# Half sums, row store, x and bz loads as items of the order lists; left rows of b by one load; head outputs of 32 columns; new lists

## The chip, the core and the metric

The kernel runs on one core of one Trainium2 chip. The metric is device time in microseconds; the median of the runs counts. TensorE (PE) multiplies, ScalarE (ACT) and VectorE (DVE) move and transform tiles, GpSimd (POOL) copies in SBUF, SyncE (SP) and, in the first part, ACT issue DMAs. PEld in the profile is the weight load of TensorE.

## What is computed

Branch A is attention with a recurrent memory: the sequence of 2048 rows (640 wide) is cut into 64 segments of 32 rows. Each segment is put behind 8 memory rows, and the first 8 rows of its output are the memory of the next one, so the 64 segments are a chain. Branch B is a gated feed-forward layer over all rows, and a gate per row mixes the two.

```python
for s in range(n_seg):
    xs = x[:, s * seg_len:(s + 1) * seg_len, :]
    h = concatenate([mem, xs], axis=1)            # 8 + 32 rows
    q, k, v = h @ Wq, h @ Wk, h @ Wv              # 32 heads of 192
    p = softmax(where(mask, q @ k.T * scale, -1e9))
    o = (p @ v) @ Wo                              # summed over heads
    mem = o[:, :M, :]
    outs.append(o[:, M:, :])
g = sigmoid((x * gate_w).sum(-1))
return g * a + (1 - g) * ((gelu(x @ w_gate) * (x @ w_up)) @ w_down)
```

All tensors are bf16.

## The kernel before

First the feed-forward part runs in four blocks of 512 rows: transposes of x, gate and up projections (L849, L852), down projection (L867, L870). Its result goes to `b_scr` in HBM, 128 rows at a time, from `brow` (store L881, on ACT's queue). The transposed x and the row gates go to HBM too. Then `segment(s)` runs 64 times.

A segment works on 32 columns, the 8 memory rows and the first 24 of its own rows. Its last 8 rows ("left" rows) can't change the memory, so they are done for four segments at once: their Q and K by "lf" items ahead of time, through HBM (`qkl`, stores L950 and L955, loads L1000 into the space of the `uT` buffers), their V (`vl`) too, and their output by `wo_left` in every fourth segment. So the score tiles have 40 columns, `R` = 32 + 8.

The 32 heads are four groups ("octets") of eight. The order of a segment's work is written out in `PROGS`, one list for each of s % 4 (called list 0 to 3 here). Each engine works its own instructions in the order in which the items add them; `_Sched` derives the waits. It also makes reads of one PSUM bank by two engines wait for each other. The items:

- ("g", n, k): projections of group n of `GROUPS`, k-th of five slices of the depth, sets of four 32-column matmuls (L1121, or L226 where the weights stay). After the last slice ACT evacuates the Q and K rows (L1141) and V (L1144).
- ("tq", i), ("tk", i): DVE transposes those rows (L1155).
- ("sc", i): mask and scores (L1163, L1171, L1176), maximum and subtraction on DVE (L1189, L1191); GpSimd then fills the left columns of Q and K for the next group (L1006, L1008).
- ("ex", i): exponent on ACT (L1201), sum, reciprocal and p on DVE (L1203 to L1208).
- ("pt", i): transposes of p (L1221, L1226) and their evacuation (L1239; for the last group L1233 on ACT and L1235 on DVE).
- ("pv", i): `pv_oct`, p times V (L1254, L1256); ACT copies the 40-column head outputs to `uT` (L1265), for the last group two thirds of them, while DVE copies the rest (L1270); GpSimd copies their 8 left columns on to `uTl` (L1273).
- ("wo", i, h): `wo_part`, output projection (L1283 into bank OB for groups 0 to 2, L1306 for the last). After ("wo", 2, 1) `half_sums` adds the two halves of the bank: ACT copies one half (L1289), DVE adds (L1292, twice). The gate column of the segment is read by ACT (L1039) after that or after "pv" of the last group, whichever item is later.
- ("lf", q, u, k), ("le", q, u, m): projections of left rows (L936, L226) and their evacuation by ACT (L941) and transpose by DVE (L943). ("vb", k): V of left rows (L1094).

At a segment's end DVE adds the last projection to the half sums (L1468) and transposes the memory rows into the next h (L1472); the next segment's first projections wait for that. `mix` (L1048, L1050) makes the output row in `bz`.

Around the lists, SP issues in this order: each weight piece that is swapped is loaded right behind the item that used its place (`swap_loads`, L645; L642 for the piece `HALF`, of which only `HX` bytes a partition are swapped); `out_store` (L1021) and `x_load` (L751) after K's last slice of group 1; `bz_load` (L1012) and, every fourth segment, `bzl_load` in four parts (L1017) after the last "g". `x_copy` (L802, GpSimd) puts the loaded x in place after the last "g".

## Time and profile before

| | |
|---|---|
| median of 3 runs | 1715.51 us (1715.17 to 1721.14) |
| the profiled execution | 1721.14 us, span 1719.3 us |
| granted TensorE clock | 0.996 |
| feed-forward part | to about 170 us |
| segments: first to last transpose of the memory rows (L1472), 62 segments | 205.9 to 1688.6 us, 23.9 us each |
| DMA | 484.99 MB, mean 282 GB/s |

In the page, busy time is the union of an engine's instructions. In the table of waits, a row names the engine and the line that waited, and the engine and line that released it. In the timeline a row has the start, the length, the engine, the line and the number of instructions merged; in brackets stands the idle time of the engine before it and its releaser. In the groups, busy time and mean length in ns come first behind the bar, then idle time of the engine before them.

### The profile page before, as it was taken

How to read it: one execution, taken by the hardware profiler on the slowest of the kernel's cores; microseconds unless marked ns; L12 is line 12 of the kernel's file. 1: busy time of each engine (PE TensorE's matmuls, PEld its weight loads, DVE VectorE, ACT ScalarE, POOL GpSimd, SP SyncE). 2: the span in 40 equal slices, each digit the busy share in tenths (PEclk: the TensorE clock that was granted, in tenths of full speed). 3: DMA queues.
4: the chain of work that ended last, by engine and by line, in shares of the span. 5: the costliest groups of instructions: out<-in, count | busy, mean ns of one | idle time of the engine just before them, and what ended most of it. 6: DMA issues, size and time to landing. Idle time of an engine off the chain costs nothing. (4 is left out here: it accounts for less than half of the span.)

```text
span 1719.3 us, 80494 instructions
## 1 busy us (share of the span) xinstructions
PE 1592.6 (93%) x39181; PEld 825.5 (48%) x31501; DVE 956.2 (56%) x2930; ACT 801.1 (47%) x1899; POOL 415.7 (24%) x1101
## 2 busy tenths in 40 slices
...
GB/s 323 319 53 137 322 299 291 320 278 285 276 303 318 278 293 282 298 304 298 280 280 290 311 299 272 290 280 320 255 288 279 314 312 269 291 265 322 274 275 240
DMA packets 273822, 484.99 MB, mean 282 GB/s; under 512 B 107686, under 2 KB 142782, under 8 KB 273470
## 3 DMA queue, kind: packets, MB, share of 16 engines
...
## 5 line engine op out<-in xcount | busy, mean ns | idle before, releaser
L1121 PE MATMUL ps<-arena 128*32 128x384 bf16 x9940 | 710.8, 329 | 20.6 <-DVE arena L1472 11.8
L226 PE MATMUL ps<-arena 128*32 128x384 bf16 x7680 | 595.3, 327 | 14.3 <-ACT arena L1039 4.4
L1121 PEld LDWEIGHTS ps<-arena 128*32 128x32 bf16 x9940 | 254.7, 96 | 392.7 <-issue 260.6
L1155 DVE STREAM_TRANSPOSE arena<-arena 128x384 bf16<-128x384 bf16 x512 | 275.3, 561 | 151.4 <-ACT arena L1141 149.8
L1141 ACT ACTIVATE arena<-ps 128x384 bf16<-128x384 f32 x512 | 237.1, 490 | 227.0 <-PE ps L1121 212.2
L1283 PE MATMUL ps<-arena 128*32 128x320 bf16 x6144 | 279.7, 301 | 15.5 <-issue 13.2
L1273 POOL COPY arena<-arena 128x96 bf16<-128x96 bf16 x256 | 163.8, 640 | 527.8 <-ACT arena L1265 480.9
L1265 ACT ACTIVATE arena<-ps 128x480 bf16<-128x480 f32 (+1 forms) x256 | 137.5, 537 | 172.3 <-PE ps L1256 160.5
L1283 PEld LDWEIGHTS ps<-arena 128*32 128x32 bf16 x6144 | 169.3, 107 | 72.9 <-issue 23.8
L1006 POOL COPY arena<-arena 128x96 bf16<-128x96 bf16 x256 | 68.9, 269 | 485.4 <-PE ps L1176 387.4
L1144 ACT ACTIVATE arena<-ps 128x384 bf16<-128x384 f32 x256 | 125.2, 489 | 104.9 <-PE ps L1121 101.6
L1189 DVE TENSOR_REDUCE arena<-ps 104x4 f32<-104x160 f32 x256 | 82.8, 323 | 141.9 <-PE ps L1176 125.1
L1203 DVE TENSOR_REDUCE arena<-ps 104x4 f32<-104x160 f32 x256 | 80.9, 316 | 103.8 <-ACT ps L1201 101.5
L1239 ACT ACTIVATE arena<-ps 128x448 bf16<-128x448 f32 x192 | 104.1, 542 | 65.9 <-PE ps L1226 64.9
L1254 PE MATMUL ps<-arena 128*64 128x160 bf16 x1536 | 118.8, 243 | 7.3 <-ACT arena L941 3.2
L1201 ACT ACTIVATE ps<-ps 104x160 f32<-104x160 f32 x256 | 74.8, 292 | 103.0 <-DVE ps L1191 103.0
L1254 PEld LDWEIGHTS ps<-arena 128*64 128x64 bf16 x1536 | 79.8, 109 | 86.4 <-issue 29.9
L936 PE MATMUL ps<-arena 128*32 128x384 bf16 x1280 | 109.4, 327 | 1.1 <-issue 1.1
L1256 PE MATMUL ps<-arena 128*64 128x64 bf16 x1536 | 102.3, 193 | 0.0
L943 DVE STREAM_TRANSPOSE arena<-arena 128x384 bf16<-128x384 bf16 x128 | 73.0, 571 | 44.2 <-ACT arena L941 43.9
L1171 PE MATMUL ps<-arena 128*40 128x40 bf16 x2048 | 68.9, 182 | 26.4 <-DVE arena L1155 24.5
L1306 PE MATMUL ps<-arena 128*32 128x160 bf16 x3072 | 71.7, 233 | 21.7 <-DVE arena L1270 16.4
...
## 6 DMA issues: line engine op xcount, KB each, us to landing
...
arena<-in_A_Wo_dram SPq DMA_DIRECT2D x205, 480.0 KB, 5.4
...
arena<-left_qk_scratch SPq DMA_DIRECT2D x126, 96.0 KB, 2.1
...
left_qk_scratch<-arena SPq DMA_DIRECT2D x30, 96.0 KB, 3.3
```

What stands on the lines that cost most here:

```text
L226: return e.add_instruction(mybir.InstMatmult(name=nm, start_tensor_calc=like["start"], stop_tensor_calc=stop, tile_size=(128, 32), tile_po ...
L936: fns.append(lambda e, outp=outp, rhs=rhs, j=j: e.matmul(outp, lhs, rhs, start=(k == 0), stop=(k == KT - 1), tile_position=(0, 32 * j)))
L1121: fns.append(lambda e, outp=outp, rhs=rhs, j=j: e.matmul(outp, lhs, rhs, start=(k == 0), stop=(k == KT - 1), tile_position=(0, 32 * j)))
L1141: S_.add("act", lambda e, m=m, bk=bk: e.activation(out=rows_sb[m], in_=ps[:, bk, 0:384], func=ACTF.Copy), reads=[r_ps[bk]], writes=[r_rows ...
L1144: S_.add("act", lambda e, i=i, bk=bk: e.activation(out=v_sb[i % NVB].rearrange("p (c n) -> p c n", c=3), in_=ps[:, bk, 0:384].rearrange("p ...
L1155: S_.add("dve", lambda e: e.transpose(out=dst[:, :, 0:L], in_=rows_sb[m].rearrange("p (c r) -> p c r", r=L)), reads=[r_rows[m]], writes=[r ...
L1239: S_.add("act", lambda e: e.activation(out=PT, in_=ps[:, bank, 0:PTW + 128], func=ACTF.Copy), reads=[r_ps[bank]], writes=[r_PT], name="pT ...
L1254: return [lambda e: e.matmul(full, v[:, e0:e0 + 64], PTm[:, i], start=True, stop=False, tile_position=(0, 64 * i), skip_group_check=True), ...
L1256: lambda e: e.matmul(part, vl[:, e0:e0 + 64], PTl[:, i], start=False, stop=True, tile_position=(0, 64 * i), skip_group_check=True)]
L1265: S_.add("act", lambda e: e.activation(out=apx(u[:, 0, 0, :], [[R, na], [3 * R, 4], [1, R]]), in_=ps[:, A, 0:na * W].rearrange("p (c t r) ...
L1273: S_.add("pool", lambda e: e.tensor_copy(out=uTl[:, q, :, 12 * oc:12 * oc + 12].rearrange("p i (t c) -> p t c i", c=3), in_=u[:, :, :, L:R ...
L1283: fns.append(lambda e, i=i, t=t, j=j, gv=gv: e.matmul(ps[32 * j:32 * j + 32, bank, 0:2 * DJ].rearrange("p (h n) -> p h n", h=2), lhs2[i], ...
```

## The change

`half_sums` is cut in two: `half_part` (ACT's copy) is item ("zp", 0), the sums by DVE are item ("zs", 0). The row store is item ("ou", 0), the x load ("xt", 0), the loads of bz and bzl ("bz", 0). All four lists are new. The `uT` buffers hold 32 columns; the 8 left columns go from PSUM to `uTl` by DVE, and GpSimd's copy is gone. The 384 bytes a partition that this frees keep more of `HALF` in place. In the feed-forward part the left rows of b are also stored to `bl_scr`, four DMAs for 128 rows, so that `bzl_load` is one DMA. The gate's buffer shares the place of `xls`. The lists 0 and 3 of before are cut to their ends here.

```diff
     b_scr = nc.dram_tensor("ffn_b_scratch", (S, Dm), BF, kind="Internal").ap()
+    bl_scr = nc.dram_tensor("ffn_bl_scratch", (NG, 4, 32, DJ), BF, kind="Internal").ap()
     x_scr = nc.dram_tensor("x_scratch", (NSEG, 128, KT * XA), BF, kind="Internal").ap()
...
-    wsB["uT"] = al(NUB * 12 * R * 2)
+    wsB["uT"] = NUB * 12 * L * 2
...
-    UB = 12 * R * 2
-    uT = [bview(wsB_off["uT"] + b * UB, UB).rearrange("p (t c r) -> p t c r", c=3, r=R) for b in range(NUB)]
+    UB = 12 * L * 2
+    uT = [bview(wsB_off["uT"] + b * UB, UB).rearrange("p (t c r) -> p t c r", c=3, r=L) for b in range(NUB)]
...
-    fp_sz = {"xst": 16 * KT * XA * 2, "xls": 4 * KT * 64, "gr": 512, "gwT": 64}
+    fp_sz = {"xst": 16 * KT * XA * 2, "xls": 4 * KT * 64, "gwT": 64}
-    o_gr = fp_off["gr"]
+    o_gr = fp_off["xls"]
...
     PROGS = [
-         ("lf", 0, 1, 2), ("ex", 3), ("pv", 2), ("lf", 0, 1, 3), ("g", 6, 2), ("g", 6, 3), ("g", 6, 4), ("pt", 3),
-         ("lf", 0, 1, 4), ("le", 0, 1, 0), ("wo", 1, 0), ("wo", 1, 1), ("pv", 3), ("wo", 2, 0), ("le", 0, 1, 1),
-         ("wo", 2, 1), ("wo", 3, 0), ("wo", 3, 1)],
...
-        [("lf", 1, 0, 0), ("lf", 1, 0, 1), ("g", 0, 0), ("g", 0, 1), ("g", 0, 2), ("g", 0, 3), ("g", 0, 4),
-         ("lf", 1, 0, 2), ("tk", 0), ("lf", 1, 0, 3), ("lf", 1, 0, 4), ("tq", 0), ("g", 1, 0), ("le", 1, 0, 0),
-         ("g", 1, 1), ("sc", 0), ("g", 1, 2), ("g", 1, 3), ("le", 1, 0, 1), ("g", 1, 4), ("tq", 1), ("tk", 1),
-         ("g", 2, 0), ("g", 2, 1), ("g", 2, 2), ("g", 2, 3), ("ex", 0), ("g", 2, 4), ("g", 3, 0), ("g", 3, 1),
-         ("lf", 1, 1, 0), ("sc", 1), ("pt", 0), ("g", 3, 2), ("g", 3, 3), ("g", 3, 4), ("g", 4, 0), ("g", 4, 1),
-         ("ex", 1), ("pv", 0), ("tk", 2), ("g", 4, 2), ("tq", 2), ("g", 4, 3), ("g", 4, 4), ("lf", 1, 1, 1),
-         ("pt", 1), ("sc", 2), ("tq", 3), ("g", 5, 0), ("g", 5, 1), ("g", 5, 2), ("g", 5, 3), ("lf", 1, 1, 2),
-         ("wo", 0, 0), ("ex", 2), ("g", 5, 4), ("pv", 1), ("tk", 3), ("sc", 3), ("g", 6, 0), ("lf", 1, 1, 3),
-         ("pt", 2), ("wo", 0, 1), ("g", 6, 1), ("g", 6, 2), ("ex", 3), ("lf", 1, 1, 4), ("pv", 2), ("g", 6, 3),
-         ("pt", 3), ("g", 6, 4), ("wo", 1, 0), ("le", 1, 1, 0), ("wo", 1, 1), ("pv", 3), ("le", 1, 1, 1),
-         ("wo", 2, 0), ("wo", 2, 1), ("wo", 3, 0), ("wo", 3, 1)],
-        [("lf", 2, 1, 0), ("g", 0, 0), ("g", 0, 1), ("g", 0, 2), ("g", 0, 3), ("g", 0, 4), ("tk", 0), ("g", 1, 0),
-         ("g", 1, 1), ("g", 1, 2), ("tq", 0), ("g", 1, 3), ("g", 1, 4), ("sc", 0), ("g", 2, 0), ("tq", 1),
-         ("g", 2, 1), ("g", 2, 2), ("ex", 0), ("g", 2, 3), ("g", 2, 4), ("g", 3, 0), ("g", 3, 1), ("lf", 2, 1, 1),
-         ("tk", 1), ("g", 3, 2), ("pt", 0), ("sc", 1), ("g", 3, 3), ("ex", 1), ("tq", 2), ("g", 3, 4), ("g", 4, 0),
-         ("g", 4, 1), ("g", 4, 2), ("g", 4, 3), ("pv", 0), ("lf", 2, 1, 2), ("tk", 2), ("pt", 1), ("lf", 2, 1, 3),
-         ("g", 4, 4), ("sc", 2), ("pv", 1), ("g", 5, 0), ("g", 5, 1), ("ex", 2), ("wo", 0, 0), ("wo", 0, 1),
-         ("lf", 2, 1, 4), ("g", 5, 2), ("g", 5, 3), ("tq", 3), ("g", 5, 4), ("tk", 3), ("g", 6, 0), ("pt", 2),
-         ("g", 6, 1), ("sc", 3), ("le", 2, 1, 0), ("ex", 3), ("wo", 1, 0), ("g", 6, 2), ("pv", 2), ("wo", 1, 1),
-         ("wo", 2, 0), ("pt", 3), ("g", 6, 3), ("g", 6, 4), ("wo", 2, 1), ("pv", 3), ("le", 2, 1, 1), ("wo", 3, 0),
-         ("wo", 3, 1)],
...
-         ("tq", 3), ("g", 5, 1), ("g", 5, 2), ("g", 5, 3), ("g", 5, 4), ("wo", 0, 0), ("pt", 2), ("tk", 3),
-         ("g", 6, 0), ("sc", 3), ("g", 6, 1), ("wo", 0, 1), ("g", 6, 2), ("pv", 2), ("wo", 1, 0), ("ex", 3),
-         ("g", 6, 3), ("wo", 1, 1), ("g", 6, 4), ("vb", 0), ("vb", 1), ("pt", 3), ("wo", 2, 0), ("pv", 3),
-         ("wo", 2, 1), ("wo", 3, 0), ("wo", 3, 1), ("vb", 2), ("vb", 3), ("vb", 4)]]
+        [("xt", 0), ("g", 0, 0), ("g", 0, 1), ("g", 0, 2), ("g", 0, 3), ("g", 0, 4), ("tq", 0), ("g", 1, 0),
+         ("g", 1, 1), ("tk", 0), ("g", 1, 2), ("sc", 0), ("ex", 0), ("g", 1, 3), ("g", 1, 4), ("ou", 0), ("g", 2, 0),
+         ("g", 2, 1), ("tk", 1), ("g", 2, 2), ("tq", 1), ("g", 2, 3), ("pt", 0), ("g", 2, 4), ("g", 3, 0), ("sc", 1),
+         ("pv", 0), ("g", 3, 1), ("g", 3, 2), ("g", 3, 3), ("g", 3, 4), ("g", 4, 0), ("wo", 0, 0), ("lf", 0, 1, 0),
+         ("g", 4, 1), ("lf", 0, 1, 1), ("g", 4, 2), ("ex", 1), ("g", 4, 3), ("tq", 2), ("tk", 2), ("g", 4, 4),
+         ("sc", 2), ("tq", 3), ("g", 5, 0), ("lf", 0, 1, 2), ("g", 5, 1), ("lf", 0, 1, 3), ("g", 5, 2), ("g", 5, 3),
+         ("g", 5, 4), ("lf", 0, 1, 4), ("tk", 3), ("pt", 1), ("g", 6, 0), ("wo", 0, 1), ("ex", 2), ("bz", 0),
+         ("pv", 1), ("sc", 3), ("le", 0, 1, 0), ("g", 6, 1), ("pt", 2), ("wo", 1, 0), ("g", 6, 2), ("ex", 3),
+         ("pv", 2), ("g", 6, 3), ("g", 6, 4), ("wo", 1, 1), ("pt", 3), ("wo", 2, 0), ("wo", 2, 1), ("zp", 0),
+         ("pv", 3), ("zs", 0), ("le", 0, 1, 1), ("wo", 3, 0), ("wo", 3, 1)],
+        [("lf", 1, 0, 0), ("lf", 1, 0, 1), ("lf", 1, 0, 2), ("g", 0, 0), ("g", 0, 1), ("g", 0, 2), ("g", 0, 3),
+         ("g", 0, 4), ("lf", 1, 0, 3), ("lf", 1, 0, 4), ("tq", 0), ("g", 1, 0), ("tk", 0), ("le", 1, 0, 0),
+         ("g", 1, 1), ("sc", 0), ("g", 1, 2), ("g", 1, 3), ("ex", 0), ("g", 1, 4), ("g", 2, 0), ("tq", 1),
+         ("g", 2, 1), ("g", 2, 2), ("le", 1, 0, 1), ("pt", 0), ("g", 2, 3), ("g", 2, 4), ("g", 3, 0), ("g", 3, 1),
+         ("tk", 1), ("g", 3, 2), ("g", 3, 3), ("g", 3, 4), ("lf", 1, 1, 0), ("sc", 1), ("pv", 0), ("g", 4, 0),
+         ("g", 4, 1), ("g", 4, 2), ("ou", 0), ("g", 4, 3), ("tk", 2), ("tq", 2), ("ex", 1), ("g", 4, 4), ("g", 5, 0),
+         ("g", 5, 1), ("sc", 2), ("g", 5, 2), ("g", 5, 3), ("pt", 1), ("g", 5, 4), ("tk", 3), ("lf", 1, 1, 1),
+         ("tq", 3), ("lf", 1, 1, 2), ("ex", 2), ("pv", 1), ("wo", 0, 0), ("g", 6, 0), ("g", 6, 1), ("sc", 3),
+         ("pt", 2), ("g", 6, 2), ("ex", 3), ("lf", 1, 1, 3), ("g", 6, 3), ("lf", 1, 1, 4), ("wo", 0, 1), ("xt", 0),
+         ("g", 6, 4), ("pv", 2), ("bz", 0), ("le", 1, 1, 0), ("wo", 1, 0), ("pt", 3), ("wo", 1, 1), ("wo", 2, 0),
+         ("wo", 2, 1), ("le", 1, 1, 1), ("zp", 0), ("pv", 3), ("wo", 3, 0), ("zs", 0), ("wo", 3, 1)],
+        [("lf", 2, 1, 0), ("lf", 2, 1, 1), ("xt", 0), ("g", 0, 0), ("g", 0, 1), ("g", 0, 2), ("g", 0, 3),
+         ("g", 0, 4), ("lf", 2, 1, 2), ("g", 1, 0), ("tq", 0), ("g", 1, 1), ("g", 1, 2), ("tk", 0), ("g", 1, 3),
+         ("g", 1, 4), ("sc", 0), ("g", 2, 0), ("g", 2, 1), ("tq", 1), ("tk", 1), ("g", 2, 2), ("ex", 0), ("g", 2, 3),
+         ("g", 2, 4), ("g", 3, 0), ("sc", 1), ("g", 3, 1), ("g", 3, 2), ("g", 3, 3), ("g", 3, 4), ("pt", 0),
+         ("lf", 2, 1, 3), ("tq", 2), ("g", 4, 0), ("g", 4, 1), ("tk", 2), ("pv", 0), ("ex", 1), ("sc", 2),
+         ("g", 4, 2), ("g", 4, 3), ("g", 4, 4), ("ou", 0), ("pt", 1), ("tq", 3), ("g", 5, 0), ("g", 5, 1),
+         ("g", 5, 2), ("g", 5, 3), ("ex", 2), ("g", 5, 4), ("lf", 2, 1, 4), ("tk", 3), ("g", 6, 0), ("wo", 0, 0),
+         ("wo", 0, 1), ("le", 2, 1, 0), ("sc", 3), ("pv", 1), ("bz", 0), ("g", 6, 1), ("pt", 2), ("ex", 3),
+         ("wo", 1, 0), ("pv", 2), ("g", 6, 2), ("g", 6, 3), ("pt", 3), ("wo", 1, 1), ("g", 6, 4), ("wo", 2, 0),
+         ("wo", 2, 1), ("zp", 0), ("pv", 3), ("zs", 0), ("wo", 3, 0), ("le", 2, 1, 1), ("wo", 3, 1)],
+        [("g", 0, 0), ("g", 0, 1), ("g", 0, 2), ("g", 0, 3), ("g", 0, 4), ("g", 1, 0), ("tq", 0), ("tk", 0),
+         ("g", 1, 1), ("g", 1, 2), ("g", 1, 3), ("sc", 0), ("ex", 0), ("g", 1, 4), ("g", 2, 0), ("tq", 1),
+         ("g", 2, 1), ("g", 2, 2), ("g", 2, 3), ("g", 2, 4), ("tk", 1), ("g", 3, 0), ("g", 3, 1), ("g", 3, 2),
+         ("g", 3, 3), ("pt", 0), ("g", 3, 4), ("g", 4, 0), ("sc", 1), ("tq", 2), ("ex", 1), ("pv", 0), ("g", 4, 1),
+         ("g", 4, 2), ("g", 4, 3), ("g", 4, 4), ("pt", 1), ("tk", 2), ("sc", 2), ("ou", 0), ("ex", 2), ("pv", 1),
+         ("tq", 3), ("g", 5, 0), ("wo", 0, 0), ("g", 5, 1), ("g", 5, 2), ("g", 5, 3), ("pt", 2), ("g", 5, 4),
+         ("wo", 0, 1), ("g", 6, 0), ("tk", 3), ("pv", 2), ("g", 6, 1), ("g", 6, 2), ("g", 6, 3), ("sc", 3),
+         ("vb", 0), ("vb", 1), ("xt", 0), ("ex", 3), ("g", 6, 4), ("wo", 1, 0), ("bz", 0), ("wo", 1, 1), ("pt", 3),
+         ("wo", 2, 0), ("pv", 3), ("wo", 2, 1), ("zp", 0), ("wo", 3, 0), ("wo", 3, 1), ("vb", 2), ("vb", 3),
+         ("vb", 4), ("zs", 0)]]
...
-    HX = 1152
+    HX = 768
...
+            for i in range(4):
+                S_.add(AUXQ, lambda e, bs=bs, row0=row0, i=i: e.dma_start(
+                    bl_scr[row0 // 128, :, M * i:M * i + M].rearrange("j r n -> r j n"),
+                    brow[bs][L * i + XA:L * i + L].rearrange("t (j n) -> t j n", j=4)),
+                    reads=[r_brow[bs]], writes=[Rg("dbl", row0 // 128, row0 // 128 + 1)], dma_sem="bl%d%d" % (bs, i), watch=True,
+                    name="bl store %d" % row0)
...
     def bzl_load(g):
-        for j in range(4):
-            S_.add(AUXQ, lambda e, j=j: e.dma_start(bzl[32 * j:32 * j + 32], rows(b_scr, g)[1][:, :, DJ * j:DJ * (j + 1)]),
-                   reads=[Rg("dr", 128 * g, 128 * g + 128)], writes=[r_bzlj[j]], dma_sem="bzl%d" % j, name="bzl load g%d" % g)
+        S_.add(AUXQ, lambda e: e.dma_start(bzl, bl_scr[g].rearrange("j r n -> (j r) n")),
+               reads=[Rg("dbl", g, g + 1)], writes=[r_bzl], dma_sem="bzl", name="bzl load g%d" % g)
...
-        S_.add("act", lambda e: e.activation(
-            out=apx(u[:, 0, 0, :], [[R, na], [3 * R, 4], [1, R]]),
-            in_=ps[:, A, 0:na * W].rearrange("p (c t r) -> p c t r", t=4, r=R), func=ACTF.Copy),
-            reads=[r_ps[A]], writes=[ru[0]] if na == 2 else ru, name="uT evac s%d o%d" % (s, o))
+        q = s % 4
+        ul = uTl[:, q, :, 12 * oc:12 * oc + 12].rearrange("p i (t c) -> p c t i", c=3)
+        pa, pb = [ps[:, b_, 0:3 * W].rearrange("p (c t r) -> p c t r", t=4, r=R) for b_ in (A, B)]
+        S_.add("act", lambda e: e.activation(out=u.rearrange("p t c r -> p c t r")[:, 0:na], in_=pa[:, 0:na, :, 0:L], func=ACTF.Copy),
+               reads=[r_ps[A]], writes=[ru[0]] if na == 2 else ru, name="uT evac s%d o%d" % (s, o))
         if na == 2:
-            S_.add("dve", lambda e: e.tensor_copy(out=u[:, :, 2, :], in_=ps[:, B, 2 * W:3 * W].rearrange("p (t r) -> p t r", r=R)),
+            S_.add("dve", lambda e: e.tensor_copy(out=u[:, :, 2, :], in_=pb[:, 2, :, 0:L]),
                    reads=[r_ps[B]], writes=[ru[1]], name="uT mid s%d o%d" % (s, o))
-        q = s % 4
-        S_.add("pool", lambda e: e.tensor_copy(
-            out=uTl[:, q, :, 12 * oc:12 * oc + 12].rearrange("p i (t c) -> p t c i", c=3), in_=u[:, :, :, L:R]),
-            reads=[r_uT[o % NUB]], writes=[r_uTl[q][oc]], name="uTl s%d o%d" % (s, o))
+            S_.add("dve", lambda e: e.tensor_copy(out=ul[:, 2], in_=pb[:, 2, :, L:R]),
+                   reads=[r_ps[B]], writes=[r_uTl[q][oc]], name="uTl mid s%d o%d" % (s, o))
+        S_.add("dve", lambda e: e.tensor_copy(out=ul[:, 0:na], in_=pa[:, 0:na, :, L:R]),
+               reads=[r_ps[A]], writes=[r_uTl[q][oc]], name="uTl s%d o%d" % (s, o))
...
-    def half_sums(bank, tag):
+    def half_part(bank, tag):
         S_.add("act", lambda e: e.activation(out=zpart[0:64], in_=ps[64:128, bank, 0:2 * DJ], func=ACTF.Copy),
                reads=[r_ps[bank]], writes=[r_zp], name="Zp " + tag)
+
+    def half_sums(bank, tag):
         for h in (1, 0):
...
-        if pairs[-1] == allp[-1]:
-            half_sums(OB, "s%d" % s)
...
     def left_sums(g):
+        half_part(LB, "left g%d" % g)
         half_sums(LB, "left g%d" % g)
         mix_left(g)
...
-                ki = [j for m, j in GROUPS[i] if m == 1 and item[2] == KT - 1]
-                kind, i = ("k", ki[0]) if ki else ("", 0)
-                if kind == "k" and i == 1:
-                    if s > 0:
-                        out_store(s - 1)
-                    if s + 1 < NSEG:
-                        x_load(s + 1)
+            elif kind == "zp":
+                half_part(OB, "s%d" % s)
+            elif kind == "zs":
+                half_sums(OB, "s%d" % s)
+            elif kind == "ou":
+                if s > 0:
+                    out_store(s - 1)
+            elif kind == "xt":
+                if s + 1 < NSEG:
+                    x_load(s + 1)
+            elif kind == "bz":
+                bz_load(s)
+                if q == 2:
+                    bzl_load(g)
...
             if n == nqkv:
-                bz_load(s)
-                if q == 2:
-                    bzl_load(g)
```

7 lines of the change are left out of this document (4 added, 3 removed), and 12 rows, old and new, of the table PROGS.

## The prediction

> **What bounds the kernel now.** I read the page first, then the table of who waited for whom on TensorE, then the timeline of one pass of lists 1 and 2 (counted from 0, as the position of the segment among four).
>
> ```profile
> span 1719.3 us, 80494 instructions
> PE 1592.6 (93%) x39181; PEld 825.5 (48%) x31501; DVE 956.2 (56%) x2930; ACT 801.1 (47%) x1899; POOL 415.7 (24%) x1101
> ```
>
> TensorE (PE) is busy for 1592.6 us and idle for 1719.3 - 1592.6 = 126.7 us. The change touches no matmul, so what it can give lies in that idle time, and what it can cost is new idle time. DVE has 763 us free in total, but it works its queue in order, so a late instruction there can still hold a matmul. The waits of TensorE, in total us, times, longest:
>
> ```profile
> PE ps L1171 <- DVE arena L1155: 24.5, 46, 0.7
> PE ps L1306 <- DVE arena L1270: 16.4, 16, 1.1
> PE ps L1121 <- DVE arena L1472: 11.8, 19, 0.8
> PE ps L1221 <- DVE arena L1208: 8.5, 17, 0.7
> PE ps L226 <- ACT arena L1039: 4.4, 12, 0.5
> PE ps L1254 <- ACT arena L941: 3.2, 15, 0.4
> PE ps L1306 <- DMA arena<-in_A_Wo_dram: 2.5, 5, 0.8
> PE ps L1254 <- ACT arena L1144: 2.4, 13, 0.2
> ```
>
> In order: scores wait for the transposed Q and K rows; the last head group's output projection waits for the third of its head outputs that DVE evacuates; the next segment's first projection waits for the new memory tokens; the transposes of p wait for p; then waits for banks and evacuations. Sixteen times means once per group of four segments, that is in one list only. The rows named come to 73.7 us.
>
> One pass of list 1 around its last scores:
>
> ```profile
> 790.38 0.34 PE L936 MATMUL ps<-arena 128*32 128x384 bf16 x4
> 790.70 0.58 PE L1283 MATMUL ps<-arena 128*32 128x320 bf16 x12
> 791.11 0.34 PE L1121 MATMUL ps<-arena 128*32 128x384 bf16 x4
> 791.38 0.26 PE L1254 MATMUL ps<-arena 128*64 128x160 bf16 x2
> 791.50 0.49 ACT L1141 ACTIVATE arena<-ps 128x384 bf16<-128x384 f32 x1 [0.66 <-PE ps L1121]
> 791.70 0.24 PE L1163 MATMUL ps<-arena 128*40 128x160 bf16 x2
> 792.02 0.58 DVE L1155 STREAM_TRANSPOSE arena<-arena 128x384 bf16<-128x384 bf16 x1
> 792.65 0.28 PE L1171 MATMUL ps<-arena 128*40 128x40 bf16 x8 [0.72 <-DVE arena L1155]
> ```
>
> Starts give the lengths: half a left item and its other half 0.32 us (0.16 a set of four matmuls), "wo" 0.41, "pv" 0.32 to 0.42. The last K set (791.11) needs evacuation, transpose and 0.05 us before the scores at 792.65: 1.54 us, of which the list covers 0.6.
>
> The end of list 2 and the start of list 3:
>
> ```profile
> 820.13 0.43 ACT L1289 ACTIVATE arena<-ps 64x320 f32<-64x320 f32 x1
> 820.16 0.26 PE L1254 MATMUL ps<-arena 128*64 128x160 bf16 x2 [0.19 <-ACT arena L1144]
> 820.59 0.67 DVE L1292 TENSOR_TENSOR arena<-ps,arena 64x160 f32<-64x160 f32 x2 [0.99 <-ACT arena L1289]
> 820.69 0.44 ACT L1265 ACTIVATE arena<-ps 128x320 bf16<-128x320 f32 x1
> 821.19 0.31 DVE L1270 CAST arena<-ps 128x160 bf16<-128x160 f32 x1
> 821.64 1.01 PE L1306 MATMUL ps<-arena 128*32 128x160 bf16 x48 [0.99 <-DVE arena L1270]
> 821.88 0.58 DVE L943 STREAM_TRANSPOSE arena<-arena 128x384 bf16<-128x384 bf16 x1 [0.39 <-ACT arena L941]
> 822.70 0.25 DVE L1468 TENSOR_TENSOR arena<-ps,arena 128x64 bf16<-128x64 f32 x1 [0.24 <-PE ps L1306]
> 823.29 0.35 PE L1121 MATMUL ps<-arena 128*32 128x384 bf16 x4 [0.63 <-DVE arena L1472]
> ```
>
> The half sums (L1289, L1292) stand in front of L1270 on DVE, so the last projection starts 1.48 us after "pv" does.
>
> **The change, part by part.**
>
> *What the lists take away.* (a) New list 1 puts, between the last K set and the last scores, two "lf", "pv", "wo" and two sets: 0.16 + 2 x 0.32 + 0.37 + 0.41 + 0.32 = 1.9 us, over the 1.54. But a Q transpose now stands behind the K one (0.58 more, 2.12 in all), so some 0.2 stays: (0.72 - 0.2) x 16 = 8 us. List 3 also gets more cover (a doubled "wo", "pv" and three sets): of the 24.5 us, 11.5 are list 1's, some 8 list 2's by the place in the list, and the remaining 5 go almost wholly, 4 taken. New list 2 has 0.16 + 0.32 + 0.16 + 0.82 = 1.5 us of cover, but its K transpose stands behind a softmax on DVE, so I leave its 8. Sum -12 (bounds 0 and -24.5). (b) In list 2 the half sums now follow "pv" on DVE. The projection then waits for ACT alone: 0.53 us after the start of "pv" (820.16 to 820.69), some 0.40 for the copy and 0.1 for the wake, against 1.48 now: -0.45 to -0.57 each, 16 times, -9 (bounds 0 and -16.4). (c) The gate column (L1039) is read before the half sums instead of behind them, and the "le" and V evacuations are further from "pv": the rows of 4.4, 3.2 and 2.4 us, -10 (bounds 0, -10). (d) List 2 starts with two "lf" instead of one, list 1 with three: of the 11.8 us, about 16 x 0.63 = 10 belong to list 3's start, which has no filler before or after; -1.5. Together -32.5.
>
> *What the lists add.* (e) Lists 0 and 1 had "pv" of the last heads two "wo" items before the last projection; now, as in list 2, it is directly in front of it. By the interval of (b), 0.53 + 0.40 + 0.1 - 0.4 (the "pv" itself) is some 0.6 us without a matmul, of which the profile would call 0.45 idle, since modelled ends reach 0.2 us beyond the next start (790.38 + 0.34 against 790.70 shows how little a gap is seen). 32 x 0.45 = +14.4 (bounds 0 and 32 x 0.6 = 19).
>
> *Head outputs of 32 columns, and the left columns by DVE.*
>
> ```profile
> L1273 POOL COPY arena<-arena 128x96 bf16<-128x96 bf16 x256 | 163.8, 640 | 527.8 <-ACT arena L1265 480.9 <-DVE arena L1270 27.2 <-PE ps L1283 7.7
> L1265 ACT ACTIVATE arena<-ps 128x480 bf16<-128x480 f32 x192 | 109.5, 571 | 129.6 <-PE ps L1256 119.5 <-POOL arena L1008 6.4 <-PE ps L1121 2.0
> L1265 ACT ACTIVATE arena<-ps 128x320 bf16<-128x320 f32 x64 | 28.0, 437 | 42.7 <-PE ps L1256 41.0
> L1141 ACT ACTIVATE arena<-ps 128x384 bf16<-128x384 f32 x512 | 237.1, 490 | 227.0 <-PE ps L1121 212.2 <-DVE arena L1060 6.8 <-DVE arena L1155 3.0
> L1468 DVE TENSOR_TENSOR arena<-ps,arena 128x96 bf16<-128x96 f32 x64 | 14.1, 220 | 0.0
> ```
>
> GpSimd loses 163.8 us that nothing on TensorE waited for (no row of its waits names L1273): 0 gained. ACT copies 384 columns instead of 480: 571 to about 490 ns. That is on the path only where the last projection waits for it: there 320 become 256, about -0.06 x 48 = -3. DVE gains 320 copies of 96 columns or fewer from PSUM: 320 x 0.22 = 70 us at most, to 60% of the span. They read the bank that ACT reads, and the scheduler makes two engines' reads of a bank follow each other, so each waits in DVE's order for ACT's copy: until 1.0 us after "pv" starts, then 0.22 us. Queued behind it are the next softmax sum, p, and the transposes that TensorE waits for (the 24.5 and 8.5 us). Walking the new lists with the durations above, I find the softmax of list 2's second group, list 1's third and list 3's second K transpose to stand directly behind such a copy with no matmul work to spare; elsewhere a "wo" or several sets lie between. 3 x 16 x 0.22 = +10.6. Bounds: below 0 is excluded, since work is only added; above, all 192 copies that are not a segment's last, 42 us.
>
> *The half sums' split, row store, x and bz loads.* They are the same instructions and DMAs. The row store and x load leave the place in front of the last V load in lists 1 and 3, which then lands sooner; TensorE hardly waits for V or K, so 0. What is late now is the x load of lists 1 and 3:
>
> ```profile
> L751 SPq DMA_DIRECT2D arena<-x_scratch x63: 471/519/3037, 188.3 to 1674.2; - x63
> DMA to landing us min/median/max: 6.0/7.9/9.0
> arena<-in_A_Wo_dram SPq DMA_DIRECT2D x205, 480.0 KB, 5.4
> arena<-left_qk_scratch SPq DMA_DIRECT2D x126, 96.0 KB, 2.1
> L1017 SPq DMA_DIRECT2D arena<-ffn_b_scratch x64: 590/605/653, 247.8 to 1683.5; - x64
> ```
>
> In list 1 a set, two "pv", four "wo", the gap of (e), the last projection and two "lf" lie behind it before the next segment's first projection needs x: 0.16 + 0.84 + 1.64 + 0.6 + 1.0 + 0.64 = 4.9 us, 0.3 of it for the copy into place. Today's 7.9 us to landing is with a dozen 384 KB weight loads in front; at the new place one or two Wo loads are, so I take 3 to 4 us (between 2.1, with next to nothing in front, and 5.4): 0 cost, with a rival below. "bz" now waits on SP for the row store, whose store is issued several us ahead; behind it stand only stage loads for the next segment: 0. One bzl load instead of four frees 3 x 0.6 us of SP in one segment of four, in front of stage loads that no matmul waits for: 0.
>
> *Left rows of b to their own scratch:* 64 stores on ACT's queue in the feed-forward part.
>
> ```profile
> 46.14 0.60 ACT L875 ACTIVATE arena<-ps 128x512 bf16<-128x512 f32 x1 [2.66 <-PE ps L870]
> 47.10 0.34 ACTq L881 DMA_DIRECT2D ffn_b_scratch<-arena  x1
> 172.54 1.19 DVE L943 STREAM_TRANSPOSE arena<-arena 128x384 bf16<-128x384 bf16 x2 [1.13 <-ACT arena L941]
> ```
>
> Four more issues at 0.35 are 1.4 us, inside ACT's 2.66 us of idleness per row block, so hidden; without that cover they would be 16 x 1.4 = 22 us. Behind the last block there is no such cover: the first left evacuation on ACT would start at about 173.2 instead of 172, and DVE's L943 and, through it, the first segment wait for that: +1.2 (bounds 0 and 1.4). The Trainium skill, "DMA: Bandwidth & Descriptors", Rules for kernel authors, says that many small transfers should be joined, since below 64 KB most of a transfer is overhead; that speaks for the one bzl load and against the 64 small stores. By it the stores could cost what they would uncovered, the 22 us; the row of 2.66 us idle says they are hidden.
>
> *HALF's swapped part shrinks from 144 to 96 KB:* 48 KB x 63 = 3 MB of 485, no wait: 0.
>
> **Sum.** -32.5 + 14.4 - 3 + 10.6 + 1.2 = -9.3, rounded to -10 us. The profiled execution took 1721.14 us (span 1719.3), the slowest of the three; so 1711 for it, and 1715.5 - 10 = 1705.5 for the median.
>
> A sentence apart: the Trainium skill, "Trainium Kernel Development and Optimization", Best Practices, says that matmul busy time misjudges the distance to the limit and that weight-load busy time is better; weight loads are busy for 48% here against 93%, so by that rule idle time understates what order can win, which would favour the rival of a larger gain.
>
> **Rivals.**
>
> *Slower, DVE becomes the holder.* The copies that wait for ACT delay every softmax and K transpose queued behind them: with all 192, +42 in place of +10.6, and the list gains of (a), which rest on DVE being free, gone: -9.3 + 31 + 12 = +34, so 1749; with half the copies -9.3 + 10 + 12 = +13, 1728. It decides where p or K is ready later than TensorE arrives. For it: DVE is behind three of the four largest waits. Against: 44% of DVE is free. I put it between, at 1735.
>
> *Slower, x comes late.* If the x load of list 1 takes the Wo loads' 5.4 us to land, and 0.3 to be copied, it is 0.8 us late, 16 times: +13; with today's 7.9, 3.3 us, +53. It decides at 4.6 us to landing. From the forecast, 1718 to 1758.
>
> *No change.* Waits move: (e) eats (b), and the weight stream holds what is left. The Wo loads of list 2 were issued from 813.92 for 1.28 us in this pass, and with 5.4 us of landing the last arrives near 820.2, 1.4 us before 821.64; instruction fetch or a slower load takes that margin. Then about 1714.
>
> *A larger gain.* (a) and (b) reach their bounds and (e) is filled by the modelled overlap: -24.5 - 16.4 - 11.5 for (a) to (d), half of (e) and of DVE's term, +7 + 5, the start +1, ACT's copy -3, in all -42. Half of the way there from -10 is 1689. For it: the waits come from fixed places in the lists; against: list 2's wait of 8 us has not got more cover on DVE.
>
> **Chances.** The forecast (1697 to 1711) 0.36; larger gain 0.18; no change 0.17; DVE 0.20; x late 0.09. Half a per cent (8.6 us) is about what this measurement can tell. The forecast's case lies below 1706.9 with some three quarters, so faster 0.27 + 0.18 = 0.45; same 0.09 + 0.15 = 0.24; slower 0.31 with the rest of "no change". The range, 1684 to 1738, leaves out the far ends of the larger gain and of the two slower rivals.
>
> **What would show it.** Right: the wait of L1306 for DVE falls from 16.4 us to near nothing and a wait of it for ACT's evacuation appears 48 times at 0.4 to 0.5; scores' wait for transposes falls from 24.5 to about 12; DVE busy near 1020 us, GpSimd near 250; the first segment starts 1.2 us later. Wrong: the wait of p's transposes (8.5 us) grows beyond 25, or GpSimd's x copy waits for x_scratch more than the once it did, or TensorE's idle time stays at 127 us.

## The result, and the profile after

The changed kernel takes 1839.63 us (median of 4 runs, 1835.52 to 1845.02), the kernel before 1716.14 us on the same chip: a ratio of 1.0708, 95% interval 1.0682 to 1.0734. The forecast was 1705.5 us with a range of 1684 to 1738. The kernel was to become faster and became slower.

Lines are 2 to 13 higher in the changed kernel: L867, L870, L881 became L869, L872, L883; L1121, L1171, L1221, L1306, L1472 became L1128, L1178, L1228, L1316, L1485. New are the stores of left rows (L887) and DVE's copies of left columns (L1280, L1282). The page of the changed kernel:

```profile
span 1833.5 us, 80517 instructions
PE 1612.1 (88%) x39162; PEld 819.4 (45%) x31501; DVE 1072.9 (59%) x3250; ACT 776.5 (42%) x1899; POOL 252.4 (14%) x845
PE   9388869998989899999998998989898989989887
PEclk9698889999999999999999999999999999999999
```

TensorE is idle for 221 us in place of 127, and the second to sixth of the 40 slices (46 us each) show where most of it is: in the feed-forward part, where every slice had a nine before. TensorE's row of the kernel before:

```profile
PE   9999999999899989899999999899898999899987
```

The transposes of the memory rows (name, shortest, median and longest in ns, first and last start) tell it in numbers:

```profile
L1485 DVE STREAM_TRANSPOSE arena<-arena x126: 247/275/300, 293.4 to 1804.8; 128x64 bf16<-128x64 bf16 x63, 128x96 bf16<-128x96 bf16 x63
```

The first stands at 293.4 us, where it was at 205.9: +87.5 up to the end of the first segment. From first to last it is 1511.4 us, where it was 1482.7: +28.7 in 62 segments, 24.38 us each in place of 23.91. The tail is 2.0 us shorter. Together 114.2, the difference of the spans.

ACT in the feed-forward part (start, length, line, instructions merged):

```profile
57.28 0.35 ACTq L883 DMA_DIRECT2D ffn_b_scratch<-arena  x1
57.66 14.80 ACTq L887 DMA_DIRECT2D ffn_bl_scratch<-arena  x4
72.50 0.60 ACT L877 ACTIVATE arena<-ps 128x512 bf16<-128x512 f32 x1 [15.58 <-DMA ffn_bl_scratch<-arena]
73.45 0.35 ACTq L883 DMA_DIRECT2D ffn_b_scratch<-arena  x1
73.83 4.52 ACTq L887 DMA_DIRECT2D ffn_bl_scratch<-arena  x4
```

The four stores of a row block take 14.80 and 4.52 us to issue, not 1.4: each of the last three waits on ACT's queue. The sixteen row blocks hold that queue for 107.5 us together, where 16 x 1.4 = 22 were counted. The table of waits carries it on from engine to engine:

```profile
ACT arena L877 <- DMA ffn_bl_scratch<-arena: 94.4, 11, 16.5
DVE arena L880 <- ACT arena L877: 110.6, 15, 16.7
PE ps L869 <- DVE arena L880: 22.0, 4, 11.7
PE ps L851 <- ACT arena L877: 19.8, 6, 9.4
PE ps L1316 <- ACT arena L1046: 25.3, 48, 0.6
PE ps L1128 <- DVE arena L1485: 19.2, 42, 1.0
PE ps L1228 <- DVE arena L1215: 15.0, 42, 0.6
PE ps L1128 <- DMA arena<-in_A_Wv_dram: 11.5, 24, 1.8
PE ps L1316 <- DMA arena<-in_A_Wo_dram: 9.9, 17, 1.9
PE ps L1178 <- DVE arena L1162: 7.5, 17, 0.5
```

In the segments the order of the waits changed as forecast: the last projection (L1316) waits for ACT 48 times, about half a microsecond each, and no longer for DVE; the scores (L1178) wait 7.5 us in place of 24.5. For the last projection the profile names the gate column's copy (L1046), which stands behind the evacuation of the head outputs (L1275) on ACT; the forecast named the evacuation. Three kinds of wait grew: for weights, from 4.2 us in all to 31.0; for the memory rows (L1128 for L1485), from 11.8 to 19.2; and of p's transposes for p (L1228 for L1215), from 8.5 to 15.0. The copies of left columns, by shape (busy us, mean ns):

```profile
L1282 DVE CAST arena<-ps 128x96 bf16<-128x96 f32 x192 | 116.8, 608 | 68.5 <-ACT arena L1275 25.9 <-PE ps L1128 21.5 <-PE ps L1233 11.7
L1282 DVE CAST arena<-ps 128x64 bf16<-128x64 f32 x64 | 29.6, 462 | 4.2
L1280 DVE CAST arena<-ps 128x32 bf16<-128x32 f32 x64 | 19.2, 299 | 0.0
L1278 DVE CAST arena<-ps 128x128 bf16<-128x128 f32 x64 | 18.7, 292 | 62.1 <-PE ps L1263 62.1
```

608 ns for 96 columns, where 220 were priced; a plain copy of 128 columns takes 292.

### The profile page after: what moved, and what is told of

It is laid out like the page before. It is cut to its first block, busy times and chain, and to the rows that moved or that the text cites. A ratio compares the mean times of both kernels' runs of the same rounds, so it can differ in the third digit from the quotient of the medians.

```text
span 1833.5 us, 80517 instructions
## 1 busy us (share of the span) xinstructions
PE 1612.1 (88%) x39162; PEld 819.4 (45%) x31501; DVE 1072.9 (59%) x3250; ACT 776.5 (42%) x1899; POOL 252.4 (14%) x845
## 3 DMA queue, kind: packets, MB, share of 16 engines
q8 instruction: 276, 4.52, 1.0%
## 4 chain that ended last, share of the span: by engine, by line
PE 58%; DMA 27%; DVE 8%; issue 3%; ACT 2%; ACTq 1%; SPq 0%; POOL 0%; DVEq 0%; POOLq 0%
PE ps L1128 17%; PE ps L226 13%; DMA arena<-in_A_Wv_dram 12%; PE ps L1291 9%; DMA ffn_bl_scratch<-arena 6%; DMA arena<-in_A_Wo_dram 5%; DMA arena<-left_x_scratch 4%; PE ps L854 3%; PE ps L851 3%; PE ps L1261 2%; PE ps L1183 2%; PE ps L944 2%; PE ps L1316 2%; DVE arena L1302 1%; PE ps L1170 1%
## 5 line engine op out<-in xcount | busy, mean ns | idle before, releaser
L1128 PE MATMUL ps<-arena 128*32 128x384 bf16 x9940 | 727.2, 329 | 44.6 <-DVE arena L1485 19.2
L226 PE MATMUL ps<-arena 128*32 128x384 bf16 x7680 | 588.5, 329 | 21.1 <-DVE arena L880 8.7
L1128 PEld LDWEIGHTS ps<-arena 128*32 128x32 bf16 x9940 | 254.8, 96 | 439.4 <-issue 249.9
L1162 DVE STREAM_TRANSPOSE arena<-arena 128x384 bf16<-128x384 bf16 x512 | 285.1, 581 | 146.4 <-ACT arena L1148 142.8
L1291 PE MATMUL ps<-arena 128*32 128x320 bf16 x6144 | 276.0, 303 | 11.3 <-issue 6.5
L1291 PEld LDWEIGHTS ps<-arena 128*32 128x32 bf16 x6144 | 174.1, 108 | 63.3 <-issue 13.3
L1282 DVE CAST arena<-ps 128x96 bf16<-128x96 f32 (+1 forms) x256 | 146.3, 572 | 72.8 <-ACT arena L1275 25.9
L1275 ACT ACTIVATE arena<-ps 128x384 bf16<-128x384 f32 (+1 forms) x256 | 118.5, 463 | 114.6 <-PE ps L1263 83.2
L1014 POOL COPY arena<-arena 128x96 bf16<-128x96 bf16 x256 | 70.5, 275 | 659.2 <-PE ps L1183 459.6
L1196 DVE TENSOR_REDUCE arena<-ps 104x4 f32<-104x160 f32 x256 | 84.4, 330 | 116.2 <-PE ps L1183 88.0
L1316 PE MATMUL ps<-arena 128*32 128x160 bf16 x3072 | 73.0, 234 | 36.2 <-ACT arena L1046 25.3
L804 POOL COPY arena<-arena 128x120 bf16<-128x120 bf16 x64 | 18.4, 287 | 584.7 <-PE ps L1128 228.2
L1198 DVE TENSOR_TENSOR ps<-ps,arena 104x160 f32<-104x160 f32 x256 | 85.1, 332 | 9.3
```

What stands on the lines that cost most here:

```text
L226: return e.add_instruction(mybir.InstMatmult(name=nm, start_tensor_calc=like["start"], stop_tensor_calc=stop, tile_size=(128, 32), tile_po ...
L1128: fns.append(lambda e, outp=outp, rhs=rhs, j=j: e.matmul(outp, lhs, rhs, start=(k == 0), stop=(k == KT - 1), tile_position=(0, 32 * j)))
L1162: S_.add("dve", lambda e: e.transpose(out=dst[:, :, 0:L], in_=rows_sb[m].rearrange("p (c r) -> p c r", r=L)), reads=[r_rows[m]], writes=[r ...
L1275: S_.add("act", lambda e: e.activation(out=u.rearrange("p t c r -> p c t r")[:, 0:na], in_=pa[:, 0:na, :, 0:L], func=ACTF.Copy), reads=[r_ ...
L1282: S_.add("dve", lambda e: e.tensor_copy(out=ul[:, 0:na], in_=pa[:, 0:na, :, L:R]), reads=[r_ps[A]], writes=[r_uTl[q][oc]], name="uTl s%d o ...
L1291: fns.append(lambda e, i=i, t=t, j=j, gv=gv: e.matmul(ps[32 * j:32 * j + 32, bank, 0:2 * DJ].rearrange("p (h n) -> p h n", h=2), lhs2[i], ...
```

## The experiments

### The stores, alone and without their chain

The kernel's scheduler, `_Sched`, makes a write wait for the last write of the same region. The four stores of a row block are all marked with one region (`Rg("dbl", row0 // 128, ...)`), although they write different rows. Theory A: so they wait for each other. First run: four regions.

```diff
-  writes=[Rg("dbl", row0 // 128, row0 // 128 + 1)]   # store i
+  writes=[Rg("dbl", row0 // 32 + i, row0 // 32 + i + 1)]
-  reads=[Rg("dbl", g, g + 1)]                        # bzl load
+  reads=[Rg("dbl", 4 * g, 4 * g + 4)]
```

> The changed kernel with one edit: the four stores of a row block's left rows are marked as writing four different parts of the scratch (they do), so none has to wait for the one before; the load of a group's 32 rows reads all four. Theory A (each store sits on ACT's queue until the one before it has landed, since all four are marked as writing the same region; that makes the feed-forward part 87.5 us longer, first memory-token transpose at 293.4 us instead of 205.9): the four issues take about 4 x 0.27 us, ACT's wait for these stores is gone, the first memory-token transpose comes at 206 to 212 us and the time is 1748 to 1760 us. Rival B (the stores are slow in themselves, 32 rows of 320 bytes each, and the row buffers or the queue wait for them whatever the marks say): ACT still waits 50 us or more and the time stays above 1800 us. Either way the segments' part stays as in the changed kernel, 24.36 us a segment against 23.93 before.

1754.88 us, ratio 1.0206 (1.0183 to 1.0229). ACT's timeline and the memory rows in that run:

```profile
43.80 0.35 ACTq L883 DMA_DIRECT2D ffn_b_scratch<-arena  x1
44.18 1.40 ACTq L887 DMA_DIRECT2D ffn_bl_scratch<-arena  x4
46.10 0.60 ACT L877 ACTIVATE arena<-ps 128x512 bf16<-128x512 f32 x1 [2.66 <-PE ps L872]
```

```profile
L1485 DVE STREAM_TRANSPOSE arena<-arena x126: 247/276/300, 209.0 to 1730.3; 128x64 bf16<-128x64 bf16 x63, 128x96 bf16<-128x96 bf16 x63
```

Now the four issues take 1.40 us and ACT waits 2.66 us for TensorE, to the hundredth the numbers of the forecast's row. Theory A holds. Second run: no such stores, four loads as before.

> The changed kernel without the left rows' own scratch: no such stores, and the left rows of b come by four loads from the scratch of all rows, as before. Theory A: feed-forward part as before (first memory-token transpose at 206 us), time 1745 to 1758 us, within 5 us of the kernel with separate regions. If the single load of the left rows is worth something in the segments, this kernel is slower than that one by more than 5 us. If the loss is not from the stores at all, it stays above 1800 us.

1752.73 us, 1.0207 (1.0191 to 1.0223): the free stores and the single load are worth nothing that these runs can tell from zero. Third run: the kernel before with the chained stores and the single load alone.

> The kernel before with only the left rows' scratch: the four stores of a row block marked as the same region, and one load of the 32 rows. Theory A: the whole cost of the stores shows here too, first memory-token transpose at 285 to 297 us, segments as before (23.93 us), 1716 + 87 = 1795 to 1810 us. If the cost in the changed kernel came from the stores together with the lists or the smaller buffers, it is well below 1795.

1803.62 us, 1.0492 (1.0450 to 1.0534): +86 us, with 23.87 us a segment. The cost belongs to the stores alone.

### Lists alone, columns alone

The kernel before with the new lists and their items (`zp`, `zs`, `ou`, `xt`, `bz`) and nothing else:

> The kernel before with the new lists, the half sums, row store, x and b loads as items of them, and nothing else: head outputs of 40 columns, left columns copied by GpSimd, four loads of the left rows. Theory C (the segments' loss of 28.7 us over 64 segments is that of the lists: weights and x wait on SP's queue, and the last projection waits for ACT): about 24.3 us a segment, 1735 to 1748 us. Rival D (the loss is DVE's 320 copies of left columns, 0.57 us each where I had priced 0.22): the lists alone give what was forecast for them, 23.7 us or less a segment, 1695 to 1710 us.

1769.53 us, 1.0296 (1.0278 to 1.0314), 21 us above even theory C's range. The changed kernel with the old lists and no stores, so that the 32-column head outputs, DVE's copies and the smaller swapped part of `HALF` remain:

> The changed kernel with the lists of the kernel before and no stores of left rows: only the head outputs of 32 columns, DVE's copies of the left columns and the smaller swapped part remain of the change. Theory C: DVE has room, 23.9 to 24.0 us a segment, 1712 to 1722 us. Rival D: the copies hold softmax and transposes, 24.3 us or more a segment, 1738 us or more. If both lists and columns lose, or only the two together, this and the lists alone both lie between.

1752.72 us, 1.0211 (1.0186 to 1.0235). Each loses by itself, and both together (1752.73) lose no more than the columns. What TensorE waits for, summed over its rows of the table of waits by releaser, in us:

| | weights | DVE | ACT | GpSimd | no reason shown ("issue") |
|---|---|---|---|---|---|
| before | 4.2 | 66.7 | 14.3 | 2.1 | 24.1 |
| lists alone | 47.0 | 30.7 | 36.4 | 16.7 | 20.9 |
| columns alone | 3.3 | 85.2 | 29.0 | 2.1 | 18.1 |
| both (no stores) | 27.7 | 47.7 | 32.9 | 2.2 | 29.6 |

The lists take 36 us off DVE's waits and put 22 on ACT's, as forecast in kind; what ruins them is 43 us of waits for weights and 15 for GpSimd. Two rows of TensorE in the run with the lists alone:

```profile
PE ps L1122 <- DMA arena<-in_A_Wk_dram: 22.7, 36, 1.3
PE ps L1284 <- POOL arena L1274: 14.5, 12, 2.5
```

SP's queue from 300 to 1700 us, in that run and then in the kernel before:

```profile
SPq L203 <- POOL arena L1274: 75.5, 30, 5.0
```

```profile
SPq L203 <- POOL arena L1273: 10.8, 22, 3.3
```

GpSimd's copies come late in the new order; SP waits for them with a load that reuses the `uT` space, and the weight loads stand behind it on the queue. By the traces they are late because x is, the rival "x comes late", though by another way than the prediction gave it. What GpSimd's copy of x waits for, in that run and then in the kernel before (one wait of some 21 us is the first load's in both):

```profile
POOL arena L803 <- DMA arena<-x_scratch: 101.5, 15, 21.1
```

```profile
POOL arena L802 <- DMA arena<-x_scratch: 20.9, 1, 20.9
```

In list 3, the load of x is issued 15.6 us after the transposes of the memory rows, where it was 8.8, and lands 6.2 us later (means over the passes, worked out from the traces). In all 12 of TensorE's waits for GpSimd, GpSimd had stood idle for 3.9 to 5.5 us and copied x within 0.15 us of that landing; the copy of the left columns stands behind it. With halved weight loads (below) x lands in 3.4 us in list 3, and TensorE's waits for GpSimd fall from 16.7 to 4.9 us. In the run with both halves, where GpSimd copies no left columns, they are 2.2, and those for weights 27.7 in place of 47.0; more than this differs there. So the chain is read from the traces, and no run moved the x load alone in these lists.

In the columns alone it is the rival "DVE becomes the holder" (scores for the transposed rows, 24.5 before):

```profile
PE ps L1135 <- DVE arena L1119: 51.7, 64, 1.7
```

### The weight stream

Theory W: the new lists ask for the last swapped weights earlier than the stream brings them. Times from the segment's start, means over the passes of a list, worked out from the landings of the loads on SP and the starts of the matmuls in the traces:

```
                          last V landed / its set   last Wo landed / last half projection
before          list 1         19.4 / 19.8               23.2 / 23.0
                list 2         18.3 / 20.1               22.2 / 23.1
own regions     list 1         18.9 / 19.1               23.6 / 23.4
                list 2         18.5 / 19.6               23.2 / 22.3
half of loads   list 1         13.5 / 18.0               21.5 / 22.3
(new lists)     list 2         12.9 / 18.9               20.1 / 21.4
```

(The last Wo piece is needed in the second half of its item.) To thin the stream, swaps load half of their columns. These kernels leave out half of each swap: the other half of each place keeps the weight that it replaces, and the output is not that of the function.

```diff
+  if name != "res":      # a swap: the left half of the columns only
+      S_.add("sp", lambda e: e.dma_start(hv(piece_view(...)), hv(piece_src(key))), ...)
```

> The changed kernel with separate regions, where each weight that is swapped in during the segments (13 of Q, K, V and 3 of Wo in each) is loaded with half of its columns only, so that the other half keeps the weight it replaces. Theory W (the new lists ask for the last V, K and Wo sets earlier than the weight stream brings them): TensorE's waits for weights, 32.6 us in the kernel with separate regions, fall below 4 us, and the time from 1754.9 to 1720 to 1730 us. Rival Q (the loss lies in what waits on the engines, the weights are only named because they come last): the waits move to others and the time stays above 1742 us.

> The kernel before with the same halved swaps. Theory W: its order leaves the weights time, 4.2 us of waits for them in all, so 1709 to 1718 us. If less traffic by itself quickens TensorE or the other engines, it falls below 1705 us, and the same amount has to be taken off what the halved loads give in the changed kernel.

The changed kernel with separate regions falls to 1668.55 us, the kernel before to 1679.83 (ratios to the kernel before with full loads 0.9706 and 0.9777). Both ranges of theory W are missed, low: less traffic quickens the kernel before by 37.5 us too, so that has to be taken off; 86.3 - 37.5 = 49 us are what the full stream costs the changed kernel beyond what it costs the kernel before. In the profiled executions the changed kernel gains 56.3 us of idle time and 35.1 of TensorE's busy time, the kernel before 23.8 and 17.2. So some 32 of the 49 us are idle time, and of these 28 are waits for weights (32.6 us gone in the one, 4.2 in the other); the rest is busy time for the same matmuls, which no run took apart. And with the halved loads the changed kernel is 11.3 us faster than the one before; the forecast's sum was -9.3. To see which of its terms were right, the two halves with halved loads:

> The lists alone (as in the run of that name) with halved swap loads, so that the other half of each swapped weight keeps the one it replaces; the kernel before took 1679.8 us so. Theory W (the lists lose to the weight stream alone): the loss of 51.7 us turns into the gain that was forecast for them, -32.5 + 14.4 = -18: 1658 to 1668 us, no waits for weights. Rival Q (they lose on the engines too, 16.7 us of waits for GpSimd and 22 more for ACT in the run with full loads): 1680 us or more.

> The columns alone (lists of before) with halved swap loads. Theory D (with the old lists the copies hold DVE whatever the weights do: scores' wait for transposes 48.1 us there): the loss of 35 us stays for the most part, 1702 to 1716 us. Rival W2 (this loss too is the weight stream's): 1680 to 1692 us, near the +7.6 us that was forecast for the columns.

| | columns of before | 32 columns, DVE copies |
|---|---|---|
| full loads, old lists | 1717.8 | 1752.7 |
| full loads, new lists | 1769.5 | 1752.7 |
| half, old lists | 1679.8 | 1716.8 |
| half, new lists | 1642.5 | 1668.6 |

(The kernel before took 1717 to 1720 us beside these.) The lists alone with halved loads lie 16 us below theory W's range, the columns alone 1 us above theory D's. With halved loads the lists gain 37 us (forecast 18) and the columns cost 37 (forecast 8). With full loads the lists lose 52. On top of the new columns the lists gain 48 us with halved loads and nothing with full ones: lists and columns don't simply add. Rival S, the places on SP's queue, with row store and x load put back ahead of the last set of the second group and the b loads behind the last set:

> The changed kernel with separate regions and the row store, x load and b load back at their old places in SP's queue (store and x load ahead of the last set of the second group, b load behind the last set), the rest of the new lists kept. Theory W says that the order of the matmuls sets the weights' waits, not these three: 1750 to 1760 us, waits for weights 28 to 37 us. Rival S (the weights are late since these items stand in front of them on SP's queue or wait there, 17.1 us for the row store): waits for weights below 15 us and 1740 us or less.

1748.63 us, 1.0190 (1.0135 to 1.0245), waits for weights 22.6 us in place of 32.6. It lies between both ranges: the three places may have a part of the lateness, and the rest is left to the order of the matmuls.

### Single steps on the old lists

Step (b) alone: half sums of list 2 behind "pv".

```diff
-        if pairs[-1] == allp[-1]:
+        if pairs[-1] == allp[-1] and s % 4 != 2:
             half_sums(OB, "s%d" % s)
...
                 pv_oct(s, i)
+                if i == NOCT - 1 and q == 2:
+                    half_sums(OB, "s%d" % s)
```

> The kernel before with one part of the change: in list 2 the half sums come behind the last head outputs (pv) instead of ahead of them. The step (b) of the prediction gave -9 us for it (the last projection's wait for DVE, 16.4 us, becomes one for ACT of about 8). Theory W agrees here, since the last Wo weight lands at 22.2 us of list 2 and is asked for at 23.1: the place has 0.9 us to give, 1706 to 1711 us. If the weights take it back, no change: 1714 to 1719 us.

1730.03 us, 1.0079 (1.0052 to 1.0106): slower, above both ranges. The end of one list 2 in its timeline:

```profile
826.38 1.01 PE L1306 MATMUL ps<-arena 128*32 128x160 bf16 x46 [0.59 <-ACT arena L1265]
826.82 0.67 DVE L1292 TENSOR_TENSOR arena<-ps,arena 64x160 f32<-64x160 f32 x2 [0.59 <-ACT arena L1289]
...
827.52 0.17 ACT L1039 ACTIVATE arena<-ps 128x2 f32<-128x2 f32 x1 [0.73 <-DVE arena L1292]
827.59 0.49 ACT L941 ACTIVATE arena<-ps 128x384 bf16<-128x384 f32 x1
...
828.13 0.25 PE L1306 MATMUL ps<-arena 128*32 128x160 bf16 x2 [0.74 <-ACT arena L941]
```

The projection starts earlier (0.59 us of wait, not 0.99), but the gate copy (L1039) now waits for the late sums, the left evacuation (L941) stands behind it on ACT, and the scheduler has hung the next operation's wait for L941 on the last two matmuls. With three moves in lists 1 to 3 added:

```diff
-  list 1: ("tk", 3), ("sc", 3), ("g", 6, 0), ("lf", 1, 1, 3),
+          ("tk", 3), ("g", 6, 0), ("lf", 1, 1, 3), ("sc", 3),
-  list 2: ("g", 6, 1), ("sc", 3), ("le", 2, 1, 0), ("ex", 3), ("wo", 1, 0),
+          ("g", 6, 1), ("le", 2, 1, 0), ("wo", 1, 0), ("sc", 3), ("ex", 3),
-  list 3: ("tk", 2), ("pt", 1), ("sc", 2), ("ex", 2), ("g", 5, 0), ("pv", 1), ("tq", 3), ("g", 5, 1),
+          ("tk", 2), ("g", 5, 0), ("g", 5, 1), ("pt", 1), ("sc", 2), ("ex", 2), ("pv", 1), ("tq", 3),
```

> The kernel before with the half sums of list 2 behind pv and three moves in its lists: in list 1 the last scores behind the first set of the last group and a left item; in list 2 the last scores behind one half of a projection; in list 3 two sets ahead of the second transposes of p. Their waits were 11.4, 8.2 and 8.2 us. Theory W: lists 2 and 3 have 0.9 and 1.6 us between the last landing and its use and give about 0.4 and 0.3 us each time, list 1 has none (last Wo landed at 23.2 us, asked for at 23.0) and gives nothing: -9 - 7 - 5 = 1693 to 1703 us. If places in the lists could be filled without regard to the weights, list 1 gives 8 more: 1685 to 1692 us.

1724.61 us, 1.0027 (1.0006 to 1.0048), again above both ranges and with the same flaw. Mended: ACT's part stays ahead of "pv", the sums go behind the gate copy.

```diff
             if item == gate_at[q]:
                 gate_now(s)
+            if q == 2 and item == ("pv", NOCT - 1):
+                half_sums(OB, "s%d" % s)
```

> The kernel before with the half sums of list 2 behind pv and also behind the gate column's copy, as in the new lists; ACT's part of them stays ahead of pv. In the run with the half sums ahead of the gate copy, that copy waited for them on ACT, the left rows' evacuation stood behind it, and the last two matmuls of the segment waited 0.74 us for that one. Theory G (this, and not the weights, ate step (b)): steps (b) and (c) together give their 9 us and more, 1704 to 1712 us. Theory W (with the waits gone the last Wo weight of list 2, 22.1 us, or the next segment's weights hold it): 1714 to 1722 us.

> The same with the three moves in lists 1, 2 and 3. Theory G: the 12 us that the flaw cost come off 1724.6 and the moves give what is left of them, 1698 to 1709 us. Theory W: 1712 to 1722 us, no better than without the moves.

1710.18 us, 0.9945 (0.9928 to 0.9962), and 1705.83 us, 0.9918 (0.9896 to 0.9941) with the moves: both beat the kernel before and lie in theory G's ranges: the gate copy, and not the weights, had eaten step (b). The last projection's wait, in the first of the two:

```profile
PE ps L1308 <- ACT arena L1039: 9.3, 17, 0.6
```

16.4 us for DVE became 9.3 for ACT. The moves gave 4 us of their 12: DVE's waits fell by 21 us more (50.7 to 30.0), waits for weights rose by 5 (7.2 to 12.6) and ACT's by 4. In all TensorE's idle time fell by 12.9 us (118.4 to 105.5), but its busy time rose by 6.3 (1591.1 to 1597.4), which is not explained.

### The price of the left columns

The copies on ACT in place of DVE, with the new lists and with the old:

> The changed kernel without the left rows' scratch, and with the copies of the left columns (128x96 and 128x32 from PSUM) on ACT in place of DVE. Theory D (DVE's queue is what the columns cost): DVE falls to some 950 us busy, its waits fall by 20 us, 1725 to 1738 us, against 1752.7 with DVE. Theory W (whatever the engines give back, the weight stream takes): 1745 us or more, with waits for weights of 35 us or more.

> The columns alone, with the copies on ACT in place of DVE. Theory D: of the 35 us that the columns cost with DVE most comes back, 1716 to 1728 us; scores' wait for transposes falls from 48 to 28 us or less. If the cost lies in the two reads of one bank following each other, whichever engine does it: 1740 us or more.

1770.88 and 1765.02 us (1.0299 and 1.0254): theory D falls, another engine pays as much. With the old lists scores' wait for transposes went back to 23.0 us, but the projections at L226 now waited 22.9 us for ACT's gate copy in place of 5.3. With the new lists the waits for weights were 30.5 us, fewer than theory W's 35. The copy of 96 columns on ACT:

```profile
L1239 ACT ACTIVATE arena<-ps 128x96 bf16<-128x96 f32 x192 | 118.8, 619 | 0.0
```

So the copy is as dear on ACT. Both runs would also fit a cost of two reads of one bank behind each other, whichever engine does them; the next run keeps those reads. From 32 to 96 columns it grows by 4.8 ns a column ((608 - 299) / 64). It walks third, head, row, and in `uTl` neighbours in a row are 48 elements apart, 96 bytes (the expectation says 192). Walked row by row it writes 12 neighbours in a run (and reads PSUM in the same new order):

```diff
-  out=ul[:, 0:na], in_=pa[:, 0:na, :, L:R]
+  out=ul[:, 0:na].rearrange("p c t i -> p i t c"), in_=pa[:, 0:na, :, L:R].rearrange("p c t i -> p i t c")
```

> The columns alone on DVE, with each copy walking its 96 columns row by row (row, then head and third, 12 neighbours written in a run) in place of third, head, row (each element written 192 bytes from the one before). The copies took 605 ns for 96 columns, 462 for 64, 298 for 32, that is 4.8 ns a column, while a plain copy of 128 columns took 292. If the order of the walk is what makes a column dear: 96 columns in 300 to 350 ns, DVE busy 980 to 1000 us, and with half of the time half of the loss: 1730 to 1742 us against 1752.7. If the price is of reading the third with a step from PSUM, whatever is written: the same 600 ns and 1748 to 1757 us.

```profile
L1239 DVE CAST arena<-ps 128x96 bf16<-128x96 f32 x192 | 48.5, 253 | 71.1 <-PE ps L1248 32.5 <-ACT arena L1232 21.3 <-PE ps L1085 10.9
```

253 ns, and 1732.30 us, 1.0098 (1.0066 to 1.0129): 20 of the 35 us are gone. Of the other 15, 14 can be read in the profile: scores still wait 38.7 us for the transposes behind DVE's copies, not 24.5.

```profile
PE ps L1135 <- DVE arena L1119: 38.7, 60, 1.4
```

The Trainium skill, "SBUF — State Buffer", Door 1, states that SBUF is fast for neighbours in one 16-byte line and pays for every step to another; the run agrees, 608 to 253 ns for the same 96 elements. Both flaws mended in the changed kernel:

> The changed kernel with both flaws mended: separate regions for the stores, and the copies row by row. What is left against the kernel before is then the new lists under the full weight stream. Theory W: the forecast's engine gains are there (DVE's waits below the 50.5 us of the kernel with separate regions alone), but waits for weights stay at 25 to 40 us and the time at 1730 to 1745 us, slower than before. If the copies were all that spoiled the lists: waits for weights below 15 us and 1718 us or less.

1749.02 us, 1.0151 (1.0123 to 1.0179). DVE's waits fell to 35.7 us, but waits for weights rose to 42.4: the stream took back what the copies gave. Theory W is right in kind, and low by a few us in both numbers.

## Why the prediction was wrong, step by step

*The premise.* "The change touches no matmul, so what it can give lies in that idle time" did not hold: some 22 of the 84 us of the stores, and 25 of the 37 us that the lists gave with halved loads, are changes of TensorE's busy time for the same matmuls.

*"Left rows of b to their own scratch": the step that failed most.* It priced the four issues, 1.4 us, and found them hidden in 2.66; both numbers stood when the stores were free. It didn't follow what the four stores write: one region, so three of four wait for a landing, 4.52 us for four in a quiet stretch and 14.80 beside weight loads. No rival had it. The first transpose of the memory rows comes 84.4 us earlier without that chain (293.4 and 209.0), where +1.2 us were forecast for the whole step. The page cited there spoke against the step, but 22 us by its rule is a quarter of the cost; that ACT would have to wait for each landing stood in the code.

*"Head outputs of 32 columns, and the left columns by DVE": a mis-sized term.* The price of 0.22 us was taken from an instruction with as many columns but neighbouring elements; it measured 0.61 for 96. +7.6 (10.6 for DVE less 3 for ACT) became +35, measured with the old lists, and with copies of 253 ns it is still +15. That the copies hold what is queued behind them on DVE was right: scores' wait rose from 24.5 to 51.7 us there. The places that the prediction walked in the new lists were not checked one by one.

*"What the lists take away", (a) to (c), and "what the lists add", (e): right in mechanism.* (a) left 7.5 us of 24.5 in the changed kernel (12 forecast); (b) with its share of (c) alone gave -10 us (-9 for (b)), and the three rows of (c) are gone in the changed kernel; (e) gave 25.3 us of waits for ACT at 48 places for (b) and (e) together (48 x 0.45 = 21.6 forecast), with the gate copy named and not the evacuation. The pair of rows cited there for an overlap of 0.2 us, 790.38 + 0.34 against 790.70, shows 0.02; the next pair, 790.70 + 0.58 against 791.11, shows 0.17. (d) was wrong: the wait for the memory rows rose from 11.8 to 19.2. With halved loads the lists gave 37 us, twice the sum, but not by its terms alone: 32 us less of waits for DVE (68.9 to 36.8) against 19 more for ACT make some 13, near the 18 that were forecast, and 25 lie in TensorE's busy time (1575.4 to 1550.7 us for the same matmuls), which no run took apart.

*What the sum left out: the stream.* "TensorE hardly waits for V or K, so 0" took today's 4.2 us of waits for weights as if they showed slack. In the old order the last Wo piece of list 1 already landed 0.2 us after the half projection that uses it had begun; the new lists with full loads wait 47.0 us for weights, with halved loads 0.3. Only the rival "No change" had this mechanism ("the weight stream holds what is left", 1.4 us of margin), and it stopped at no change; it goes past it, to +52 for the lists alone.

*Steps at nothing that held:* the single bzl load (1754.9 against 1752.7 us). The three items' places on SP cost the changed kernel at most a few us (1748.6 with the old places). `HALF`'s smaller part was not tried by itself. The sign for a late x load showed (GpSimd's copy waited for x_scratch 10 times). In the changed kernel it held TensorE little, whose waits for GpSimd stayed at 1.7 us; in the lists alone, where GpSimd still copies the left columns, it stands at the head of 14.5 us of TensorE's waits. The price was sought in list 1, before the next segment's projection; it fell in list 3, behind GpSimd.

That -9.3 was nearly the -11.3 of the runs with halved loads is chance: -37 and +37 do not even add up to it.
